# Decode attention: four batches of a kv head interleaved over the partitions in 16 KB runs, P padded with zeros, V loads among the last K loads, w4 in ten loads

## The chip, the cores and the metric

One core of one Trainium2 chip runs the whole program. The time is device microseconds of one execution. Spans in profiles are about 1.7 us shorter than the times. All comparisons are against executions of the kernel before on the same chip in the same rounds, unless a sentence says otherwise. Where one experiment's time is subtracted from another's, the two may come from different chips and rounds; the median of the kernel before lay between 224.1 and 224.8 us in all of them.

Engines are named as the profile names them: PE multiplies matrices, PEld loads its weights, DVE and ACT are the vector and scalar engines, POOL is GpSimd, and SP does nothing here but issue loads, in order.

## The reference, cut to what matters

```python
x  = A_x                                     # [4, 1, 576], bf16
xn = layernorm(x)
# A: 32 query heads, 16 kv heads, Dh = 128, a window of the last 2048 keys, batch 4
q = (xn @ wq) -> [4, 32, 1, 128]
p = softmax(q . k * Dh**-0.5)
A = (p . v) -> [4, 1, 4096] @ wo
# B: a small mixer and MLP: gelu(ln(xn) @ w1), a shift that leaves zeros at S = 1, @ w2,
#    x1 = xn + hs;  B = x1 + gelu(ln(x1) @ w3) @ w4        # w3: 576 x 4608, w4: 4608 x 576
return x + A + B
```

K and V of the window are 33.5 MB each; wq and wo are 4.7 MB each, w3 and w4 5.3 MB each, w1 and w2 together 1.3 MB. Every byte is used once, so this is a kernel of loads: 88.9 MB with the program's own instructions.

## The kernel before

A *unit* is 1 MB of K or V: one kv head, two of the four batches. In a unit, partition `(i, b)` holds 32 successive keys of one batch, which are 8 KB in one piece. K units go through a ring of 7 slots, V units through a ring of 9. SP issues all K units, then V units as slots come free; wo, w1 and w2 go over the dead K ring.

```python
NKU = 7; NVU = 9                  # ring slots of 1 MB
def kv_pairs(ring_t, slot, cache, u):
    g, pr = u // 2, u % 2
    return [(ring_t[:, slot * UE:(slot + 1) * UE],
             cache[pr:B:2, g, Sk - W:Sk, :].rearrange("b (i t) d -> i b (t d)", t=NT))]   # NT = 32
```

PE transposes K in blocks of eight 128x128 tiles (an *evacuation* by DVE or ACT moves each block from PSUM to SBUF). The scores of one kv head are 16 matmuls of 512 columns. The columns of one batch stand at every second place:

```python
# transposes: in_ is loaded as weights, the identity streams past
ins = e.transpose(tb[n % NTB][:, t, :], kring[:, u % NKU, 8 * k + t, :], ident_bf[:])
# scores: batch b in partitions 32b..32b+31 of PSUM, lhsT = the padded queries
ins = e.matmul(Sps[32*b:32*b+32, c4, :]..., lhsT=Qpad[:, g, b, :],
               rhs=ktbuf[:, n % NKT, :, bh:128:2], ...)
```

The exponentials come after the last head, all heads at once, and write P with a step of two, so that one transpose of P gives the layout that the V units have. The zeros between are set once:

```python
P_sb = sb("P_sb", [128, NT, 64, 2], BF16)            # zeroed once, by POOL
e.activation(out=P_sb[s, 8*q:8*q+8, :, bh], in_=Sps[s, q, :]..., func=Exp, ...)   # 8 of 64 x 512
ins = e.transpose(PTps[q][:, t, :], P_sb[:, 8*q+t, :, :].rearrange("p i b -> p (i b)"), ident_bf[:])
```

The w4 matmuls come last, in five groups; the first three wait for 1728, 1728 and 1152 KB of w4.

## Time and profile before

| | |
|---|---|
| time, median | 224.28 us of three executions, one of them an outlier of 335.86 us |
| span of the profile | 223.1 us |
| moved | 88.9 MB |
| K part on PE | 5.39 us per kv head, 19 to 106 us |
| last K transpose (SP then issues wo) to first V product | 104.8 to 119.0 us |
| last w4 matmuls | 209.6 to 220.9 us |

These are lines of the page's second part: 40 equal slices of the span. `PEclk` is the granted clock of PE in tenths, `DMA` the busy share of the 16 DMA engines in tenths (9 is 90% or more), GB/s what they moved.

```profile
PEclk9999999999999999999755555555587555665579
DMA  6999999999999999999999999999999999999950
GB/s 249 426 420 422 420 422 419 420 422 416 419 422 417 417 422 420 420 420 417 422 414 413 412 412 419 422 417 419 420 420 417 422 416 426 419 414 410 409 210 1
```

The DMA never pauses between the first slice and the tail (409 to 426 GB/s), so the time is bytes over rate, plus a start and a tail. Whatever engine waits in the middle costs nothing as long as this row stays full: from 107 to 119 us PE is busy for 4.2 of 12 us, and the DMA moves 417 GB/s.

These are lines of the chain of waits (start in us, duration in us, what): two heads of the K part, and the end.

```profile
30.34 1.09 PE ps L337 x16
...
35.73 1.10 PE ps L337 x15
...
179.78 29.80 DMA vring<-in_B_w_dram
209.57 0.04 issue
209.62 11.28 PE ps L423 x72
```

From 30.34 to 35.73 is one head: 5.39 us, of which the 16 score matmuls (L337) are 1.1. At the end, all 72 w4 matmuls stand behind the first piece of w4.

These are three lines of the timeline of SP (start, time until the last issue of the group, what):

```profile
86.97 7.04 SPq L159 DMA_DIRECT2D vring<-in_A_v_cache_dram  x9
104.75 0.40 SPq L159 DMA_DIRECT2D kring<-in_A_wo_dram  x1
120.00 1.39 SPq L159 DMA_DIRECT2D vring<-in_A_v_cache_dram  x2
```

Nine V loads are issued while the last seven K units are still in their slots. They and wo are what the DMA works on during the softmax.

These are the groups of the exponentials and of the score matmuls (line, engine, operation, shapes, count, busy us, mean ns of one, idle before):

```profile
L337 PE MATMUL ps<-regB,Qpad 128*32 128x512 bf16 x256 | 17.6, 392 | 4.5 <-ACT regB L327 4.5
L363 ACT ACTIVATE P_sb<-ps,negb 64x512 bf16<-64x512 f32 x8 | 6.6, 824 | 2.6 <-DVE negb L358 2.5
```

### The profile page before, as it was taken

To read this page: it belongs to the slowest core of one execution; us is meant where nothing else is said; L and a number is where in the kernel's file an instruction comes from. 1 tells how busy PE (TensorE), PEld (TensorE's weight loads), DVE (VectorE), ACT (ScalarE), POOL (GpSimd) and SP (SyncE) were. 2 spreads that over 40 slices of the span, in tenths; PEclk is the share of its full clock that TensorE was granted. 3 is DMA by queue.
4 is the path that set the end of the run, shared out by engine and by line. 5 is a ranking of instruction groups with operands and counts; after the bars stand their busy time and mean duration, and the time that the engine had idled before them with its cause. 6 is when DMAs were issued, how large, how long until landed. Compare 5 with 4: busy or idle time off the path is not lost.

```text
span 223.1 us, 6242 instructions
## 1 busy us (share of the span) xinstructions
PE 163.6 (73%) x2933; PEld 124.6 (56%) x2934; DVE 70.3 (32%) x124; ACT 62.1 (28%) x76; POOL 7.8 (4%) x14
## 2 busy tenths in 40 slices
PE   0459999999999999997267722665993435997596
PEld 0456777777777777775047722454573434576363
DVE  4803556666666556664441000051000000000000
ACT  2002555555555555555594000000200000000000
POOL 8500000000000000000000000000000000000000
PEclk9999999999999999999755555555587555665579
DMA  6999999999999999999999999999999999999950
GB/s 249 426 420 422 420 422 419 420 422 416 419 422 417 417 422 420 420 420 417 422 414 413 412 412 419 422 417 419 420 420 417 422 416 426 419 414 410 409 210 1
DMA packets 13682, 88.91 MB, mean 399 GB/s; under 512 B 1356, under 2 KB 1752, under 8 KB 4440
## 3 DMA queue, kind: packets, MB, share of 16 engines
q1 hardware_dynamic: 13640, 88.50, 96.1%
q8 instruction: 23, 0.38, 0.7%
q10 hardware_dynamic: 16, 0.01, 0.0%
q14 instruction: 3, 0.02, 0.0%
HBM read 88.49 MB, written 0.00 MB: 397 GB/s over the span
## 4 chain that ended last, share of the span: by engine, by line
DMA 43%; PE 40%; ACT 12%; issue 1%; DVE 1%; SPq 1%
DMA vring<-in_A_v_cache_dram 25%; PE ps L321 23%; DMA vring<-in_B_w_dram 13%; ACT regB L327 8%; PE ps L337 8%; PE ps L423 6%; DMA vring<-in_A_wq_dram 5%; ACT P_sb L363 3%; PE ps L402 2%; PE ps L309 1%; DVE rmax L357 1%; SPq L159 1%; PE ps L372 0%; ACT PT L379 0%; PE ps L294 0%
## 5 line engine op out<-in xcount | busy, mean ns | idle before, releaser
L321 PE MATMUL ps<-ident_bf,kring 128*128 128x128 bf16 x1024 | 66.7, 220 | 0.6 <-ACT regB L327 0.5
L321 PEld LDWEIGHTS ps<-ident_bf,kring 128*128 128x128 bf16 x1024 | 57.9, 98 | 14.1 <-issue 7.8
L328 DVE COPY regB<-ps 128x1024 bf16<-128x1024 bf16 x80 | 52.3, 687 | 36.0 <-PE ps L321 34.3
L327 ACT ACTIVATE regB<-ps 128x1024 bf16<-128x1024 bf16 x48 | 47.5, 1021 | 48.2 <-PE ps L321 48.2
L402 PE MATMUL ps<-PT,vring 128*128 128x4 bf16 x1024 | 30.6, 166 | 29.5 <-DMA vring<-in_A_v_cache_dram 26.7
L402 PEld LDWEIGHTS ps<-PT,vring 128*128 128x128 bf16 x1024 | 28.9, 103 | 33.6 <-DMA vring<-in_A_v_cache_dram 28.5
L337 PE MATMUL ps<-regB,Qpad 128*32 128x512 bf16 x256 | 17.6, 392 | 4.5 <-ACT regB L327 4.5
L513 ACT ACTIVATE h2T_sb<-ps 128x144 bf16<-128x144 f32 x1 | 0.3, 290 | 49.7 <-PE ps L507 49.7
L423 PE MATMUL ps<-kring,ORT 128*4 128x288 bf16 x64 | 13.7, 398 | 0.3 <-DVE ORT L441 0.3
L423 PE MATMUL ps<-vring,h2T_sb 128*4 128x288 bf16 x72 | 11.3, 328 | 2.6 <-DMA vring<-in_B_w_dram 2.6
L437 DVE TENSOR_TENSOR OTn<-ps,rinvB 128x64 bf16<-128x64 f32 (+2 forms) x3 | 0.6, 202 | 39.6 <-PE ps L402 39.6
L337 PEld LDWEIGHTS ps<-regB,Qpad 128*32 128x32 bf16 x256 | 5.3, 94 | 11.1 <-ACT regB L327 5.9
L423 PEld LDWEIGHTS ps<-vring,h2T_sb 128*4 128x4 bf16 x72 | 6.8, 96 | 6.8 <-DMA vring<-in_B_w_dram 2.7
L259 ACT ACTIVATE sd<-mv 4x1 f32<-4x1 f32 x3 | 0.6, 202 | 35.3 <-DVE mv L257 35.3
L423 PEld LDWEIGHTS ps<-kring,ORT 128*4 128x4 bf16 x64 | 7.0, 113 | 5.9 <-DVE ORT L441 0.4
L372 PE MATMUL ps<-ident_bf,P_sb 128*128 128x128 bf16 x32 | 4.1, 309 | 6.6 <-ACT P_sb L363 6.6
L475 DVE TENSOR_TENSOR x_bf<-ps,xn_bf 4x288 bf16<-4x288 f32 x2 | 0.9, 446 | 23.8 <-PE ps L470 23.8
L528 DVE CAST out_sb<-ps 4x288 bf16<-4x288 f32 x1 | 0.4, 446 | 24.0 <-PE ps L423 24.0
L372 PEld LDWEIGHTS ps<-ident_bf,P_sb 128*128 128x128 bf16 x32 | 3.1, 140 | 7.9 <-ACT P_sb L363 7.9
L363 ACT ACTIVATE P_sb<-ps,negb 64x512 bf16<-64x512 f32 x8 | 6.6, 824 | 2.6 <-DVE negb L358 2.5
L273 PE MATMUL ps<-ident_bf,xn_bf 4*128 4x4 bf16 x8 | 0.5, 166 | 8.8 <-DVE ragsrc L266 8.4
L498 PE MATMUL ps<-x1nT,regB 128*128 128x4 bf16 x144 | 5.2, 172 | 1.5 <-DMA regB<-in_B_w_dram 1.5
(78 smaller groups left out, 68.6 us busy)
## 6 DMA issues: line engine op xcount, KB each, us to landing
kring<-in_A_k_cache_dram SPq DMA_DIRECT2D x32, 1024.0 KB, 12.6
vring<-in_A_v_cache_dram SPq DMA_DIRECT2D x32, 1024.0 KB, 21.6
kring<-in_A_wo_dram SPq DMA_DIRECT2D x1, 4608.0 KB, 26.0
regB<-in_B_w_dram SPq DMA_DIRECT2D x4, 1152.0 KB, 27.0
vring<-in_A_wq_dram SPq DMA_DIRECT2D x4, 1024.0 KB, 7.9
vring<-in_B_w_dram SPq DMA_DIRECT2D x2, 1728.0 KB, 30.7
kring<-in_B_w_dram SPq DMA_DIRECT2D x2, 576.0 KB, 13.5
vring<-in_B_w_dram SPq DMA_DIRECT2D x1, 1152.0 KB, 30.2
```

The lines of the kernel that those rows point to most:

```text
L159: e.dma_start(o_, i_).then_inc(S[skey], 16)
L309: ins = e.matmul(ps[:, 4 + (w % NTB), :], lhsT=zeros_bf[:, 0:128], rhs=zeros_bf[:, :], start=True, stop=True)
L321: ins = e.transpose(tb[n % NTB][:, t, :], kring[:, u % NKU, 8 * k + t, :], ident_bf[:])
L327: return "act", lambda e: e.activation(out=ktbuf[:, n % NKT], in_=tb[n % NTB], func=ACTF.Copy)
L328: return "dve", lambda e: e.tensor_copy(out=ktbuf[:, n % NKT], in_=tb[n % NTB])
L337: ins = e.matmul(Sps[32 * b:32 * b + 32, c4, :].rearrange("p (t i) -> p t i", t=8), lhsT=Qpad[:, g, b, :], rhs=ktbuf[:, n % NKT, :, bh:128:2],
L357: add("dve", lambda e: e.tensor_reduce(out=rmax[:], in_=Sps, axis=AX.XY, op=ALU.max), waits=[f"SC{G - 1}"], sig="rmax", key=KS)
L363: add("act", lambda e, q=q, s=s, bh=bh: e.activation(out=P_sb[s, 8 * q:8 * q + 8, :, bh], in_=Sps[s, q, :].rearrange("p (t i) -> p t i", t ...
L372: ins = e.transpose(PTps[q][:, t, :], P_sb[:, 8 * q + t, :, :].rearrange("p i b -> p (i b)"), ident_bf[:])
L402: ins = e.matmul(o_, lhsT=vring[:, u % NVU, t, :], rhs=r_, start=(t == 0), stop=(t == NT - 1))
L423: return e.matmul(ACC[h], lhsT=lhsT, rhs=rhs, start=start, stop=stop)
L498: ins = e.matmul(H2Tps[:, n, :], lhsT=w3main[:, r, lo:hi:st], rhs=x1nT[:, r, :], start=(r == 0 and n == 0), stop=False, skip_group_check=True)
```

## The change

The intent: longer runs for the DMA. One load now brings 2 MB, one kv head of all four batches; a partition holds 64 successive keys, 16 KB in one piece. The rings become 3 and 4 slots of 2 MB. The columns of one batch in the transposed K now stand at every fourth place, and so do the values of one batch in P. To have work for the DMA during the softmax, V0 to V3 are issued among the last K loads. P moves into the space beside the transposed K, so that w3 must wait for the P transposes. w4 comes in pieces of 0.6 MB, each with its own matmuls.

The diff, cut to its core:

```diff
-NKU = 7
-NVU = 9
+NKU = 3
+NVU = 4
+V_EARLY = 4
-    NT = 32
+    NT = 64
+        def kv_src(cache, g):
+            return cache[:, g, Sk - W:Sk, :].rearrange("b (i t) d -> i b (t d)", t=NT)
+        def issue_k(g, key):          # waits for the last transpose of head g - 3
+        def issue_v(g, key):          # waits for PV of head g - 4
+        for g in range(G):
+            issue_k(g, g)
+        for g in range(V_EARLY):
+            issue_v(g, G - V_EARLY + g - 0.5)          # V0 after K11, V1 after K12, ...
+        wo_wait = f"T{8 * (G - 1) + 7}"                # the last K transpose
         ... wo, w1, w2 ...
+        for g in range(V_EARLY, G):
+            issue_v(g, KV + g)
-        ev_w3 = [... [f"SC{G - 1}"] ...]
+        ev_w3 = [... ["PTt7"] ...]                     # after V15 in SP's order
-        W4P = [(0, 3, 0), (3, 6, 2), (6, 8, 4)]
+        for c in range(8):                             # one load and one group of matmuls each
...
-                                       rhs=ktbuf[:, n % NKT, :, bh:128:2],
+                        ins = e.matmul(Sps[32 * b:32 * b + 32, c4, :], lhsT=Qpad[:, g, b, :], rhs=kt[:, b:2048:B],
...
-        for q in range(4):
-            for bh in range(2):              # out=P_sb[s, 8q:8q+8, :, bh], 64 x 512
+        for q in range(2):
+            for b in range(B):               # 32 x 1024
+                    out=P_sb[s, 32 * q:32 * q + 32, :, b], in_=Sps[s, 2 * q:2 * q + 2, :]...
...
-        for q in range(4):                   # P transposes, 32 in 4 groups
+        for q in range(8):                   # 64 in 8 groups
```

More of the change, by code (lines that the diff above doesn't have):

```diff
@@ L19 @@
 N_WARM = 6
-WO_AFTER = 9
-W12_AFTER = 11
+PT_ACT = (5, 7)
 AO_CH = ((0, 4), (4, 7), (7, 8))
@@ L46, in bass_parallel_sum__sliding_block_cached__mixer_s_mlp__decode_kernel @@
     G = Hkv
-    NU = 2 * G
-    NT = 32
+    NT = 64
     UE = NT * 128
-    NHB = 4 * NU
+    NHB = 8 * G
     scale = float(Dh) ** -0.5
@@ L68, in bass_parallel_sum__sliding_block_cached__mixer_s_mlp__decode_kernel @@
         W3E = 4 * F + FH
-        regB_t = sb("regB", [128, max(NKT * 1024, W3E)], BF16)
+        PE_ = 8192
+        regB_t = sb("regB", [128, max(NKT * 1024 + PE_, W3E)], BF16)
+        P_sb = regB_t[:, NKT * 1024:NKT * 1024 + PE_].rearrange("p (t i b) -> p t i b", t=NT, b=B)
         kring = kring_t[:].rearrange("p (s t d) -> p s t d", s=NKU, t=NT)
@@ L114, in bass_parallel_sum__sliding_block_cached__mixer_s_mlp__decode_kernel @@
         negb = sb("negb", [128, 1], FP32)
-        rs4 = sb("rs4", [128, 4], FP32)
+        rs2 = sb("rs2", [128, 2], FP32)
         rsum = sb("rsum", [128, 1], FP32)
@@ L118, in bass_parallel_sum__sliding_block_cached__mixer_s_mlp__decode_kernel @@
         rinvB = sb("rinvB", [128, 128], FP32)
-        P_sb = sb("P_sb", [128, NT, 64, 2], BF16)
         PT = sb("PT", [128, NT, 128], BF16)
@@ L167, in bass_parallel_sum__sliding_block_cached__mixer_s_mlp__decode_kernel @@
         KV = KS + 4.0
-        KT = KV + NU + 8.0
+        KT = KV + 2 * G + 8.0
         P = lambda *a, **k: add("pool", *a, **k)
@@ L177, in bass_parallel_sum__sliding_block_cached__mixer_s_mlp__decode_kernel @@
         P(lambda e: e.memset(Qpad_t[:], 0.0), sig="qpad_zero", key=-96)
-        P(lambda e: e.memset(P_sb[:], 0.0), sig="p_zero", key=-95)
+        P(lambda e: e.memset(P_sb, 0.0), sig="p_zero", key=-95)
         P(lambda e: e.memset(ident_f[:], 1.0), sig="if1", key=-94)
@@ L191, in bass_parallel_sum__sliding_block_cached__mixer_s_mlp__decode_kernel @@
         ev_wq.append(add_dma([(wqrag, rag_src(A_wq))], ("wq", 4), (), -15))
-        def kv_pairs(ring_t, slot, cache, u):
-            g, pr = u // 2, u % 2
-            return [(ring_t[:, slot * UE:(slot + 1) * UE],
-                     cache[pr:B:2, g, Sk - W:Sk, :].rearrange("b (i t) d -> i b (t d)", t=NT))]
-        def last_unit(nslots, s_lo, s_hi):
-            return max(u for u in range(NU) if s_lo <= u % nslots <= s_hi)
-        for u in range(NU):
-            ev_k.append(add_dma(kv_pairs(kring_t, u % NKU, A_k_cache, u), ("k", u % NKU),
-                                [f"T{4 * (u - NKU) + 3}"] if u >= NKU else [], u))
@@ L204, in bass_parallel_sum__sliding_block_cached__mixer_s_mlp__decode_kernel @@
-        wo_wait = f"T{4 * last_unit(NKU, 0, (_o - 1) // UE) + 3}"
-        for u in range(NU):
-            kk = KS + 0.01 * u
-            w = [f"PV{u - NVU}"] if u >= NVU else (["q"] if u < WQ_SLOTS else [])
-            ev_v.append(add_dma(kv_pairs(vring_t, u % NVU, A_v_cache, u), ("v", u % NVU), w, kk))
-            if u == WO_AFTER - 1:
-                ev_wo = add_dma([(wo_sb.rearrange("p h r n -> p h (r n)"), A_wo.rearrange("(h p r) n -> p h (r n)", h=8, r=4))],
-                                "wo", [wo_wait], kk + 0.005)
-            if u == W12_AFTER - 1:
-                ev_w1 = add_dma([(w1main, B_w1[0:512, :].rearrange("(p r) n -> p r n", r=4)), (w1rag, rag_src(B_w1))], "w1",
-                                [wo_wait], kk + 0.005)
-                ev_w2 = add_dma([(w2main, B_w2[0:512, :].rearrange("(p r) n -> p r n", r=4)), (w2rag, rag_src(B_w2))], "w2",
-                                [wo_wait], kk + 0.006)
+        def kv_src(cache, g):
+            return cache[:, g, Sk - W:Sk, :].rearrange("b (i t) d -> i b (t d)", t=NT)
@@ new lines, in issue_k @@
+        def issue_k(g, key):
+            w = [f"T{8 * (g - NKU) + 7}"] if g >= NKU else []
+            ev_k.append(add_dma([(kring_t[:, g % NKU * UE:(g % NKU + 1) * UE], kv_src(A_k_cache, g))], ("k", g % NKU), w, key))
+        def issue_v(g, key):
+            w = [f"PV{g - NVU}"] if g >= NVU else (["q"] if g < WQ_SLOTS else [])
+            ev_v.append(add_dma([(vring_t[:, g % NVU * UE:(g % NVU + 1) * UE], kv_src(A_v_cache, g))], ("v", g % NVU), w, key))
+        for g in range(G):
+            issue_k(g, g)
@@ new lines, in bass_parallel_sum__sliding_block_cached__mixer_s_mlp__decode_kernel @@
+        for g in range(V_EARLY):
+            issue_v(g, G - V_EARLY + g - 0.5)
+        wo_wait = f"T{8 * (G - 1) + 7}"
+        ev_wo = add_dma([(wo_sb.rearrange("p h r n -> p h (r n)"), A_wo.rearrange("(h p r) n -> p h (r n)", h=8, r=4))],
+                        "wo", [wo_wait], KS)
+        ev_w1 = add_dma([(w1main, B_w1[0:512, :].rearrange("(p r) n -> p r n", r=4)), (w1rag, rag_src(B_w1))], "w1", [], KS + 0.1)
+        ev_w2 = add_dma([(w2main, B_w2[0:512, :].rearrange("(p r) n -> p r n", r=4)), (w2rag, rag_src(B_w2))], "w2", [], KS + 0.2)
@@ L217, in bass_parallel_sum__sliding_block_cached__mixer_s_mlp__decode_kernel @@
+        for g in range(V_EARLY, G):
+            issue_v(g, KV + g)
         w3_src = B_w3[0:512, :].rearrange("(p r) n -> p r n", r=4)
-        ev_w3 = [add_dma([(w3main[:, r, :], w3_src[:, r, :])], ("w3", r), [f"SC{G - 1}"], KT + r) for r in range(4)]
-        ev_w3.append(add_dma([(w3rag, rag_src(B_w3))], ("w3", 4), [f"SC{G - 1}"], KT + 4))
+        ev_w3 = [add_dma([(w3main[:, r, :], w3_src[:, r, :])], ("w3", r), ["PTt7"], KT + r) for r in range(4)]
+        ev_w3.append(add_dma([(w3rag, rag_src(B_w3))], ("w3", 4), [], KT + 4))
@@ L224, in bass_parallel_sum__sliding_block_cached__mixer_s_mlp__decode_kernel @@
         ev_w4 = []
-        s4 = (NU - NVU) % NVU
-        assert all((s4 + s_) % NVU + 2 <= NVU for s_ in (0, 2, 4))
-        W4P = [(0, 3, 0), (3, 6, 2), (6, 8, 4)]
-        for n, (c0, c1, s_) in enumerate(W4P):
-            o0 = (s4 + s_) % NVU * UE
-            v = vring_t[:, o0:o0 + (c1 - c0) * 4 * D].rearrange("p (c rn) -> p c rn", c=c1 - c0)
-            ev_w4.append(add_dma([(v, w4_main[:, c0:c1, :])], ("w4", n), [f"PV{NU - NVU + s_ + 1}"], KT + 5 + n))
-            for c in range(c0, c1):
-                for q in range(4):
-                    w4tile[4 * c + q] = v[:, c - c0, q * D:(q + 1) * D]
-        o0 = (s4 + 4) % NVU * UE + 2 * 4 * D
-        assert 2 * 4 * D + 4 * D <= 2 * UE
+        W4N = []
+        for c in range(8):
+            g = G - NVU + c // 3
+            o0 = g % NVU * UE + c % 3 * 4 * D
+            v = vring_t[:, o0:o0 + 4 * D]
+            ev_w4.append(add_dma([(v, w4_main[:, c, :])], ("w4", c), [f"PV{g}"], KT + 5 + c))
+            W4N.append((4 * c, 4 * c + 4))
+            for q in range(4):
+                w4tile[4 * c + q] = v[:, q * D:(q + 1) * D]
+        o0 = (G - NVU + 2) % NVU * UE + 2 * 4 * D
         v3 = vring_t[:, o0:o0 + 3 * D]
         v1 = vring_t[:, o0 + 3 * D:o0 + 4 * D]
-        wl = [f"PV{NU - NVU + 5}"]
-        ev_w4.append(add_dma([(v3, w4_t3)], ("w4", 3), wl, KT + 8))
-        ev_w4.append(add_dma([(v1, w4_t1)], ("w4", 4), wl, KT + 9))
+        ev_w4.append(add_dma([(v3, w4_t3)], ("w4", 8), [], KT + 13))
+        ev_w4.append(add_dma([(v1, w4_t1)], ("w4", 9), [], KT + 14))
         for q in range(3):
@@ L244, in bass_parallel_sum__sliding_block_cached__mixer_s_mlp__decode_kernel @@
         w4tile[35] = v1
-        W4N = [(12 * n, 12 * n + 12) for n in range(2)] + [(24, 32), (32, 35), (35, 36)]
+        W4N += [(32, 35), (35, 36)]
         ev_o = [None, None]
@@ L315, in pe_T @@
         def pe_T(n):
-            u, k = n // 4, n % 4
+            g, k = n // 8, n % 8
             def f(e):
@@ L320, in f @@
                 for t in range(8):
-                    ins = e.transpose(tb[n % NTB][:, t, :], kring[:, u % NKU, 8 * k + t, :], ident_bf[:])
+                    ins = e.transpose(tb[n % NTB][:, t, :], kring[:, g % NKU, 8 * k + t, :], ident_bf[:])
                 return ins
@@ L333, in f @@
                 for c4 in range(4):
+                    n0 = (8 * g + 2 * c4) % NKT
+                    kt = regB_t[:, n0 * 1024:(n0 + 2) * 1024]
                     for b in range(B):
-                        n = 8 * g + 4 * (b % 2) + c4
-                        bh = b // 2
-                        ins = e.matmul(Sps[32 * b:32 * b + 32, c4, :].rearrange("p (t i) -> p t i", t=8), lhsT=Qpad[:, g, b, :],
-                                       rhs=ktbuf[:, n % NKT, :, bh:128:2],
+                        ins = e.matmul(Sps[32 * b:32 * b + 32, c4, :], lhsT=Qpad[:, g, b, :], rhs=kt[:, b:2048:B],
                                        start=(g == 0), stop=(g == G - 1), tile_position=(0, 32 * b))
@@ L343, in bass_parallel_sum__sliding_block_cached__mixer_s_mlp__decode_kernel @@
         for n in range(NHB):
-            w = [ev_k[n // 4]] if n % 4 == 0 else []
+            w = [ev_k[n // 8]] if n % 8 == 0 else []
             if n == 0:
@@ L359, in bass_parallel_sum__sliding_block_cached__mixer_s_mlp__decode_kernel @@
             waits=["rmax"], sig="negb", key=KS + 0.05)
-        for q in range(4):
-            for bh in range(2):
-                s = slice(64 * bh, 64 * bh + 64)
-                add("act", lambda e, q=q, s=s, bh=bh: e.activation(
-                    out=P_sb[s, 8 * q:8 * q + 8, :, bh], in_=Sps[s, q, :].rearrange("p (t i) -> p t i", t=8), func=ACTF.Exp,
-                    bias=negb[s, 0:1], scale=scale, accum_out=rs4[s, q:q + 1]),
-                    waits=["negb", "p_zero"], sig=f"exp{q}" if bh else None, key=KS + 0.1 + 0.01 * q + 0.001 * bh)
+        for q in range(2):
+            for b in range(B):
+                s = slice(32 * b, 32 * b + 32)
+                add("act", lambda e, q=q, s=s, b=b: e.activation(
+                    out=P_sb[s, 32 * q:32 * q + 32, :, b], in_=Sps[s, 2 * q:2 * q + 2, :].rearrange("p c (t i) -> p (c t) i", t=16),
+                    func=ACTF.Exp, bias=negb[s, 0:1], scale=scale, accum_out=rs2[s, q:q + 1]),
+                    waits=["negb", "p_zero"], sig=f"exp{q}" if b == B - 1 else None, key=KS + 0.1 + 0.01 * q + 0.001 * b)
         def pe_PT(q):
@@ L371, in f @@
                 for t in range(8):
-                    ins = e.transpose(PTps[q][:, t, :], P_sb[:, 8 * q + t, :, :].rearrange("p i b -> p (i b)"), ident_bf[:])
+                    ins = e.transpose(PTps[q % 4][:, t, :], P_sb[:, 8 * q + t, :, :].rearrange("p i b -> p (i b)"), ident_bf[:])
                 return ins
             return f
-        for q in range(4):
-            add("pe", pe_PT(q), waits=[f"exp{q}"] + ([f"E{NHB - 1 - k}" for k in range(NTB)] + ["xn2T"] if q == 0 else []),
-                sig=f"PTt{q}", key=KS + 0.2 + 0.01 * q)
-            if q == 3:
-                add("act", lambda e: e.activation(out=PT[:, 24:32, :], in_=PTps[3], func=ACTF.Copy), waits=["PTt3"], sig="PT3", key=KS + 0.3)
+        for q in range(8):
+            w = [f"exp{q // 4}"] + ([f"E{NHB - 1 - k}" for k in range(NTB)] + ["xn2T"] if q == 0 else [])
+            add("pe", pe_PT(q), waits=w + ([f"PT{q - 4}"] if q >= 4 else []), sig=f"PTt{q}", key=KS + 0.2 + 0.01 * q)
+            if q in PT_ACT:
+                add("act", lambda e, q=q: e.activation(out=PT[:, 8 * q:8 * q + 8, :], in_=PTps[q % 4], func=ACTF.Copy),
+                    waits=[f"PTt{q}"], sig=f"PT{q}", key=KS + 0.3 + 0.01 * q)
             else:
-                add("dve", lambda e, q=q: e.tensor_copy(out=PT[:, 8 * q:8 * q + 8, :], in_=PTps[q]), waits=[f"PTt{q}"],
+                add("dve", lambda e, q=q: e.tensor_copy(out=PT[:, 8 * q:8 * q + 8, :], in_=PTps[q % 4]), waits=[f"PTt{q}"],
                     sig=f"PT{q}", key=KS + 0.3 + 0.01 * q)
-        add("dve", lambda e: e.tensor_reduce(out=rsum[:], in_=rs4[:], axis=AX.X, op=ALU.add), waits=["exp3"], sig="rsum", key=KS + 0.5)
+        add("dve", lambda e: e.tensor_reduce(out=rsum[:], in_=rs2[:], axis=AX.X, op=ALU.add), waits=["exp1"], sig="rsum", key=KS + 0.5)
         add("dve", lambda e: e.reciprocal(out=rinv[:], in_=rsum[:]), waits=["rsum"], sig="rinv", key=KS + 0.51)
@@ L387, in bass_parallel_sum__sliding_block_cached__mixer_s_mlp__decode_kernel @@
         add("pe", lambda e: e.matmul(rinvps, lhsT=ones_f[:], rhs=diag[:], start=True, stop=True), waits=["diag", "ones_f"],
-            sig="rinvp", key=KV + 2.5)
+            sig="rinvp", key=KV + 3.5)
         add("dve", lambda e: e.tensor_copy(out=rinvB[:].rearrange("p (g b e) -> p g b e", b=B, e=2),
@@ L391, in bass_parallel_sum__sliding_block_cached__mixer_s_mlp__decode_kernel, with pe_PV @@
             waits=["rinvp"], sig="rinvB", key=KS + 0.6)
-        def pe_PV(u):
-            g, pr = u // 2, u % 2
-            o_ = OTps(g)[:, 8 * g:8 * g + 8].rearrange("p (bh b e) -> p bh b e", bh=2, b=2)[:, :, pr, :]
+        def pe_PV(g):
             def f(e):
@@ L400, in f @@
                 for t in range(NT):
-                    r_ = PT[:, t, :].rearrange("p (bh b r) -> p bh b r", bh=2, b=2)[:, :, pr, 2 * g:2 * g + 2]
-                    ins = e.matmul(o_, lhsT=vring[:, u % NVU, t, :], rhs=r_, start=(t == 0), stop=(t == NT - 1))
-                return ins
-            return f
-        for u in range(NU):
-            add("pe", pe_PV(u), waits=[ev_v[u]] + ([f"PT{q}" for q in range(4)] if u == 0 else []),
-                sig=f"PV{u}", key=KV + u)
+                    r_ = PT[:, t, :].rearrange("p (b r) -> p b r", b=B)[:, :, 2 * g:2 * g + 2]
+                    ins = e.matmul(OTps(g)[:, 8 * g:8 * g + 8].rearrange("p (b e) -> p b e", e=2), lhsT=vring[:, g % NVU, t, :], rhs=r_,
+                                   start=(t == 0), stop=(t == NT - 1))
+                return ins
+            return f
+        for g in range(G):
+            add("pe", pe_PV(g), waits=[ev_v[g]] + ([f"PT{q}" for q in range(8)] if g == 0 else []), sig=f"PV{g}", key=KV + 2 * g + 1)
         def pe_sel(a, z):
@@ L438, in bass_parallel_sum__sliding_block_cached__mixer_s_mlp__decode_kernel @@
                                                            in1=rinvB[:, 16 * a:16 * z], op=ALU.mult),
-                waits=["rinvB", f"PV{4 * z - 1}"], sig=f"OTn{n}", key=kk + 0.2)
+                waits=["rinvB", f"PV{2 * z - 1}"], sig=f"OTn{n}", key=kk + 0.2)
             add("pe", pe_sel(a, z), waits=[f"OTn{n}"] + ([f"ORT{n - 1}"] if n else []), sig=f"sel{n}", key=kk + (0.3 if last else 1.3))
@@ L449, in pe_t1 @@
             return ins
-        KH = KV + 11.5
+        KH = KV + 9.5
         add("pe", pe_t1, waits=["t1", "ident_f"], sig="t1acc", key=KH + 5.1)
```

## The prediction

> **What bounds the kernel now.** The DMA engines. The page's DMA row is at 9 tenths in every slice but the first and the tail, 410 to 426 GB/s: 88.9 MB at 418 GB/s is 213 us of 223.1. In the K part (19 to 106 us in the chain of waits) PE, at 5.39 us per kv head (64 transposes, 16 score matmuls), is slower than the DMA at about 5.0, but nothing is lost: seven K and nine V slots keep the queue full. The softmax gap, 107 to 119 us in the timeline, is hidden too: 105 to 125 us still moves 408 to 421 GB/s. At the end w4 part 0 releases PE at 209.6 us, and 72 matmuls (11.3 us) run to 220.9.
>
> **Gains.**
> 1. Longer runs. Single packets in the trace took 159 ns (4096 B), 181 (4608 B), 312 (8192 B): about 6 ns plus 0.0373 ns per byte. Estimate for 16 KB: 618 ns, against 624 for two of 8 KB. Over all K and V: about 2 us.
> 2. w4 in pieces: its matmuls start about 2 us earlier relative to w3, but the DMA itself finishes only 2 to 3 us before PE today. Worth 1 to 2 us.
>
> **Costs: the DMA queue runs dry.** The SP queue is in order, and K has only three slots of 2 MB.
> - From about K7 each K load waits for its slot (5.39 against 4.95 us per head): 2 us idle.
> - V0 to V3 go between K11 and K15, so K12 to K15 arrive 10 us apart and PE starves: K15 lands near 116 us; today the last K is transposed by 105.8. PE in bursts will partly run at half clock: [...] this trace agrees (1.00 in the K part, 0.50 in the V part).
> - Behind K15 stands wo, which waits for the last transpose, and nothing else is queued: 5 to 8 us of transposes and about 1.5 us from issue to first bytes (first issue 0.81 us; the 0 to 5 us window implies bytes from 2.3). About 9 us idle.
> - wo, w1 and w2 are 15 us of work (6.05 MB). V4 waits for PV0. From the last transpose: eviction and scores 2.5, max 2.5, eight exponentials of 1024 columns at about 1.3 (0.87 now for 512) 10.4, last four groups of P transposes and the copy 5.2 (2.1 now), PV0 2.0, issue 1.5: 24 us. About 8 us idle.
> Total 19 to 20 us of idle DMA, all on the critical path, since from V4 on all is DMA again.
> - The P_sb memset doubles (3.5 to 7 us) and holds the first layernorm's tensor_scalar on DVE (3.51 us today, 0.42 the second time): K starts near 20 us, harmless.
>
> **Prediction.** 224.3 + 20 - 2 - 2 = about 239 us (rounded), range 231 to 246. Faster by over 2%: 0.03; within 2%: 0.07; slower by over 2%: 0.90.
>
> **What would show it.** About 420 GB/s except two holes: one after K15, near 115 to 125 us, one before PV0 ends, near 140 to 148 us; SP waiting on transposes and PV; PV starting near 144 us instead of 119; 16 KB packets at 618 ns; the last w4 matmul about 1 us after its landing.
>
> **What would make it wrong.** 16 KB packets off the line; PE at full clock for K12 to K15 (3 us better); score matmuls slower with a stride of four (8-byte steps), which no view shows; a shorter softmax.

2, 9 and 8 us of idle DMA, 19 to 20 in all, less 2 and 2 for the gains, on 224.3 came to about 239 us. That PE would run partly at half clock in K12 to K15 was an estimate of mine; the trace before has a granted clock of 1.00 in the K part and 0.50 in most of the V part.

## The result, and the profile after

| | before | after |
|---|---|---|
| time, median | 224.77 us | 258.1 us (257.91 to 258.40, 4 runs) |
| ratio | | 1.150, 95% interval 1.145 to 1.155 |
| span of the profile | 223.1 us | 256.5 us |
| K part on PE, per head | 5.39 us | 6.31 us |
| last K transpose (SP then issues wo) | 104.8 us | 131.3 us |
| one exponential and its accumulator read | 0.87 us for 512 columns | 2.52 us for 1024 |
| first V product | 119.0 us | 162.2 us |

A ratio is the mean time of one kernel's fast runs over that of the other's of the same rounds, so it is not quite the ratio of the medians quoted. The 224.77 is the median of four executions with the outlier of 335.86 us among them; the three others have a mean of 224.4, and the ratio is taken against these. The direction was as predicted, the size was not: 33 us longer, where I had said 15.

The same three lines of the page's slices, after:

```profile
PEclk9999999999999999797798555555556855575569
DMA  7999998888889999999039900299999999999991
GB/s 272 420 443 427 416 386 340 327 328 335 327 332 358 416 442 416 439 419 434 28 108 420 405 13 0 82 422 427 429 424 432 422 432 416 430 413 416 410 396 58
```

There are three shortfalls where I had predicted two holes and a trickle. From the sixth slice to the thirteenth the rate is 327 to 386 instead of 420. The two holes, in the 20th and 21st slice and from the 24th to the 26th, are where I had placed them by cause, later and the second twice as long.

The stretches of the trace (stretch, its length, busy us and instructions of PE, PEld, DVE, ACT and POOL, granted clock, DMA share, GB/s) give their size:

```profile
20.00:97.00 77.00, 73.92 (x969) 49.22 (x972) 39.93 (x61) 36.22 (x37) 0.00 (x0) 1.00 0.91 369
120.00:125.00 5.00, 2.07 (x32) 1.58 (x30) 1.47 (x3) 1.84 (x2) 0.00 (x0) 1.00 0.46 193
125.00:130.00 5.00, 5.00 (x60) 3.33 (x58) 2.07 (x3) 1.47 (x2) 0.00 (x0) 0.66 0.00 0
150.00:165.00 15.00, 7.23 (x147) 6.73 (x145) 3.24 (x7) 10.59 (x9) 0.00 (x0) 0.50 0.00 1
170.00:235.00 65.00, 42.70 (x982) 32.48 (x983) 4.80 (x17) 1.72 (x4) 0.00 (x0) 0.58 1.01 426
```

With 425 GB/s as the full rate of the new loads, the K part lost 77 x (1 - 369/425) = 10 us. The first hole is 10 us (2.7 in 120 to 125, 5 in 125 to 130, 2.4 in the next five), the second 17.5 (2.3, 15.0 and 0.3). That is 38 us of idle DMA. The span grew by 33, so about 4 us were gained, as I had summed the gains. The miss lies in the idle time, 38 against 19 us.

The chain of waits, one head of the K part, then K15 landing:

```profile
33.37 2.02 PE ps L332 x16
...
39.68 2.02 PE ps L332 x16
...
101.73 22.64 DMA kring<-in_A_k_cache_dram
```

The 16 score matmuls (now L332) take 2.02 us, 0.92 more than before, with the same arithmetic, the same 512 columns and the same granted clock of 1.00. That is exactly the growth of the head, from 5.39 to 6.31. K15 took 22.6 us from issue to landing, because V3 and other loads stood before it (with V0 to V3 behind K15, in e5, PE waited 0.2 us for K loads in the whole run, against 9.1 us here).

The groups of score matmuls and exponentials after the change:

```profile
L332 PE MATMUL ps<-regB,Qpad 128*32 128x512 bf16 x256 | 32.2, 632 | 3.8 <-ACT regB L322 3.8
L357 ACT ACTIVATE regB<-ps,negb 32x1024 bf16<-32x1024 f32 x8 | 20.1, 2517 | 3.5 <-DVE negb L352 3.4
```

An exponential of twice the columns takes three times as long. The timeline of SP after the change:

```profile
101.73 0.54 SPq L159 DMA_DIRECT2D kring<-in_A_k_cache_dram  x1
131.29 0.40 SPq L159 DMA_DIRECT2D kring<-in_A_wo_dram  x1
164.03 45.60 SPq L159 DMA_DIRECT2D vring<-in_A_v_cache_dram  x12
```

wo is issued when the last transpose is done, and V4 when PV0 is done. From there to the end of the span are 256.5 - 164.0 = 92.5 us. This number returns in every experiment that keeps the order of the loads, so the whole question is when V4 is issued.

### The profile page after: what moved, and what is told of

Read it like the earlier page. It is cut to its first block, busy times and chain, and to the rows that moved or that the text cites. A ratio compares the mean times of both kernels' runs of the same rounds, so it can differ in the third digit from the quotient of the medians.

```text
span 256.5 us, 6269 instructions
## 1 busy us (share of the span) xinstructions
PE 182.7 (71%) x2966; PEld 130.3 (51%) x2966; DVE 75.7 (30%) x127; ACT 76.7 (30%) x77; POOL 11.3 (4%) x14
## 4 chain that ended last, share of the span: by engine, by line
DMA 40%; PE 40%; ACT 15%; SPq 2%; issue 1%; DVE 1%
PE ps L316 18%; DMA kring<-in_A_k_cache_dram 15%; DMA vring<-in_A_v_cache_dram 14%; DMA regB<-in_B_w_dram 11%; PE ps L332 11%; ACT regB L357 8%; ACT regB L322 6%; PE ps L415 5%; PE ps L394 4%; SPq L159 2%; PE ps L366 1%; DVE rmax L351 1%; PE ps L499 1%; ACT PT L373 0%; PE ps L382 0%
## 5 line engine op out<-in xcount | busy, mean ns | idle before, releaser
L316 PE MATMUL ps<-ident_bf,kring 128*128 128x128 bf16 x1024 | 69.8, 225 | 9.5 <-DMA kring<-in_A_k_cache_dram 9.1
L316 PEld LDWEIGHTS ps<-ident_bf,kring 128*128 128x128 bf16 x1024 | 60.4, 101 | 30.8 <-issue 13.9
L394 PE MATMUL ps<-PT,vring 128*128 128x8 bf16 x1024 | 29.2, 168 | 22.1 <-DMA vring<-in_A_v_cache_dram 20.9
L332 PE MATMUL ps<-regB,Qpad 128*32 128x512 bf16 x256 | 32.2, 632 | 3.8 <-ACT regB L322 3.8
L357 ACT ACTIVATE regB<-ps,negb 32x1024 bf16<-32x1024 f32 x8 | 20.1, 2517 | 3.5 <-DVE negb L352 3.4
L366 PE MATMUL ps<-ident_bf,regB 128*128 128x128 bf16 x64 | 7.2, 313 | 19.3 <-ACT regB L357 19.3
L366 PEld LDWEIGHTS ps<-ident_bf,regB 128*128 128x128 bf16 x64 | 6.7, 149 | 20.5 <-ACT regB L357 20.5
L332 PEld LDWEIGHTS ps<-regB,Qpad 128*32 128x32 bf16 x256 | 6.1, 106 | 16.8 <-issue 12.0
L415 PE MATMUL ps<-kring,ORT 128*4 128x288 bf16 x64 | 12.6, 377 | 0.3 <-DVE ORT L433 0.3
L376 DVE COPY PT<-ps 128x1024 bf16<-128x1024 bf16 x6 | 4.2, 692 | 19.7 <-PE ps L366 19.7
L178 POOL MEMSET regB<- 128x8192 bf16 x1 | 6.9, 6915 | 0.0
```

Source lines behind the costliest of these rows:

```text
L178: P(lambda e: e.memset(P_sb, 0.0), sig="p_zero", key=-95)
L316: ins = e.transpose(tb[n % NTB][:, t, :], kring[:, g % NKU, 8 * k + t, :], ident_bf[:])
L332: ins = e.matmul(Sps[32 * b:32 * b + 32, c4, :], lhsT=Qpad[:, g, b, :], rhs=kt[:, b:2048:B], start=(g == 0), stop=(g == G - 1), tile_posit ...
L357: add("act", lambda e, q=q, s=s, b=b: e.activation(out=P_sb[s, 32 * q:32 * q + 32, :, b], in_=Sps[s, 2 * q:2 * q + 2, :].rearrange("p c (t ...
L366: ins = e.transpose(PTps[q % 4][:, t, :], P_sb[:, 8 * q + t, :, :].rearrange("p i b -> p (i b)"), ident_bf[:])
L376: add("dve", lambda e, q=q: e.tensor_copy(out=PT[:, 8 * q:8 * q + 8, :], in_=PTps[q % 4]), waits=[f"PTt{q}"], sig=f"PT{q}", key=KS + 0.3 + ...
```

## The experiments

**Theory A.** The mechanism of the prediction is right: the SP queue is in order, three K slots are few, K15 is late, and nothing stands behind it. Only two terms were mis-sized, both for one reason, a step of four elements (8 bytes) where the kernel before had two (4 bytes): the read of the score matmuls, and the write of the exponentials. **Rivals.** B: the 16 KB packets themselves are slow, or the ring alone explains it. C: the exponentials are slow because they use 32 partitions, or because one reads two PSUM banks.

A caution about results: the comparison with the reference called every run correct, even the one that is wrong (e2). Why it sees no error in e2 was not looked into; perhaps the attention term is too small in the output. So the mended layouts below rest on index arithmetic, given with each, and not on the comparison.

### e1: the score matmuls read runs of 32

The transpose of K streams an identity past the loaded tile (a step of 64 in the tile of the P transposes, in e4, lengthens their weight loads, 176 against 149 ns after the change, and not the matmuls, 314 against 313), so a permuted identity permutes the columns of the result for nothing (64 transposes take 4.14 us with either, where PE does not wait). Column `32 b + i` of the new matrix has its one in row `4 i + b`, which is the partition of key group i of batch b. The scores come out in the same order as before.

```diff
+        pv_ = perm_bf[:].rearrange("p (b i) -> p b i", b=B)
+        affine_select(out=pv_, in_=pv_, fill=0.0, pattern=[[-1, B], [-B, 32]], channel_multiplier=1)
-   e.transpose(tb[n % NTB][:, t, :], kring[:, g % NKU, 8 * k + t, :], ident_bf[:])
+   e.transpose(tb[n % NTB][:, t, :], kring[:, g % NKU, 8 * k + t, :], perm_bf[:])
-   rhs=kt[:, b:2048:B]
+   rhs=kt.rearrange("p (t b i) -> p b t i", t=16, b=B)[:, b]
```

> The K transposes use a permuted identity, so that the score matmuls read runs of 32 columns in place of every fourth column; the result stays right. Theory A (two of my terms were mis-sized: the stride-4 read of the score matmuls, which makes a group of 16 take 2.02 us instead of 1.10, and the exponentials, 2.52 us each instead of 1.3): a group falls to about 1.1 us, the K period from 6.31 to 5.39 us per kv head, the last K transpose moves from 131 to about 122 us, and the time falls by 8 to 10 us to about 249 us. Rival B (the K ring of three slots alone, or slower 16 KB packets, holds the K part): the group time falls but the period stays above 6 us and the total stays within 2 us of 258.

Measured: 249.06 us (248.07 to 250.51), ratio 1.112 (1.107 to 1.117). A group of 16 score matmuls takes 1.05 us, the period of a head is 5.34 us, and wo is issued at 122.74 us instead of 131.29. All three numbers of theory A hold; rival B falls for this term. From V4's issue (154.2) to the end of the span (246.3) are 92.1 us.

### e2: the steps one by one (wrong on purpose)

Heads 0 to 3 read with step 4, the next four with step 2, then step 1, then runs of 32. The eight exponentials write with eight patterns.

```diff
+   r_ = (kt[:, b:2048:B], kt[:, b % 2:1024:2], kt[:, 512*b:512*b+512], <runs of 32>)[g // 4]
+   exponentials of 1024: out step 4 | step 2 | step 1 | runs of 32;  of 512: step 4 | 2 | 1 | 8
```

> Result wrong on purpose; one look. The score matmuls read their 512 columns with step 4 in heads 0 to 3, step 2 in heads 4 to 7, step 1 in heads 8 to 11 and runs of 32 in heads 12 to 15; the eight exponentials write with different steps, four of 1024 columns (step 4, step 2, step 1, runs of 32) and four of 512 columns (step 4, 2, 1, 8). Theory A1 (an 8-byte step is the cost): step 4 takes 2.0 us per 16 score matmuls, the other three 1.1 us; an exponential of 1024 columns takes 2.5 us with step 4 and about 1.3 us with the three others, and of 512 columns about 1.3 us with step 4 and 0.87 us with step 2 and step 1. Rival A2 (the 32 partitions, or the two PSUM banks read by one instruction, make the exponential slow): all four of 1024 columns take about 2.5 us whatever the step.

Measured, one look, so the state of the run is unknown; the durations are of single instructions of one trace. The timeline of PE, one group of each pattern in the order step 4, step 2, step 1, runs of 32:

```profile
45.19 2.02 PE L337 MATMUL ps<-regB,Qpad 128*32 128x512 bf16 x16 [0.22 <-ACT regB L322]
51.50 1.09 PE L337 MATMUL ps<-regB,Qpad 128*32 128x512 bf16 x16 [0.22 <-ACT regB L322]
73.06 1.05 PE L337 MATMUL ps<-regB,Qpad 128*32 128x512 bf16 x16 [0.22 <-ACT regB L322]
91.43 1.05 PE L337 MATMUL ps<-regB,Qpad 128*32 128x512 bf16 x16
```

The timeline of ACT, the four exponentials of 1024 columns in the order of the diff (the accumulator reads between them are left out):

```profile
131.40 2.51 ACT L372 ACTIVATE regB<-ps,negb 32x1024 bf16<-32x1024 f32 x1 [2.45 <-DVE negb L357]
...
133.93 1.39 ACT L372 ACTIVATE regB<-ps,negb 32x1024 bf16<-32x1024 f32 x1
...
135.38 1.10 ACT L372 ACTIVATE regB<-ps,negb 32x1024 bf16<-32x1024 f32 x1
...
136.58 1.11 ACT L372 ACTIVATE regB<-ps,negb 32x1024 bf16<-32x1024 f32 x1
```

The four of 512 columns that follow take 1.39 us (step 4), 0.83 (step 2), 0.68 (step 1) and 2.52 (step 8).

Theory A holds, and rival C falls: on the same 32 partitions and the same two banks, 1024 columns take 1.10 us in one piece and 2.51 with step 4. The two sizes give the cost of one more column: 0.82 ns at step 1, 1.09 at step 2, 2.19 at step 4 (differences of the 1024 and the 512 column times, over 512). For the writes of ACT even step 2 is not free (1.39 against 1.10 us for 1024 columns). For the reads of the matmuls step 2 nearly is (1.09 against 1.05 us), and step 4 nearly doubles the time (2.02 us). Runs of 32 and step 4 read out of the same stretch of 2048 columns (1.05 and 2.02 us), so the length of the stretch is not the cause.

### e3: exponentials in runs of 32, alone

A first version with P in the order `(t, b, i)` did not build. So P is laid out as `(i, b, t)`: an exponential writes runs of 32 along t, and the transpose loads its columns with a step of 64, in the order `(i, b)` that the V loads have. The exponential now reads its scores in steps.

```diff
-   P_sb = ....rearrange("p (t i b) -> p t i b", t=NT, b=B)
+   P_sb = ....rearrange("p (i b t) -> p i b t", t=NT, b=B)
-   out=P_sb[s, 32 * q:32 * q + 32, :, b], in_=Sps[...].rearrange("p c (t i) -> p (c t) i", t=16)
+   out=P_sb[s, :, b, 32 * q:32 * q + 32], in_=Sps[...].rearrange("p c (t i) -> p i (c t)", t=16)
-   in_=P_sb[:, 8 * q + t, :, :].rearrange("p i b -> p (i b)")
+   in_=P_sb[:, :, :, 8 * q + t].rearrange("p i b -> p (i b)")
```

> Only the layout of P changes: each exponential writes runs of 32 and reads its scores in step instead, and the P transposes load their columns with a step of 64; the result stays right. Theory A: an exponential takes 1.1 to 1.3 us instead of 2.52, the time from the last K transpose to the first V product falls from 31 to about 21 us, the hole in the DMA before V4 shrinks by the same 10 us, and the time falls to about 248 us. Rival: another wait opens (the stepped reads of scores or of P cost as much), and the time stays above 254 us.

Measured: three fast runs of 245.88 to 247.97 us (the median with the slow one is 247.46), ratio 1.102 (1.097 to 1.107). The profiled run was a slow one (250.48 us), so no stage times are compared from it, but the instructions are plain: an exponential takes 1.11 us. Theory A holds.

### e4: both strides out

> Both strides taken out at once (permuted identity for K, runs of 32 for P). Theory A: these two terms are all that my sum had wrong, so the time is what I predicted for the change, 239 us, plus or minus 2; the two DMA holes behind K15 and before V4, 15 to 17 us together, stay. Rival: the queue order was mis-sized as well, and the time lies outside 236 to 242 us.

Measured: 239.58 us (238.54 to 241.70), ratio 1.070 (1.064 to 1.076). These are its groups of score matmuls and exponentials, two lines of SP, and the K part in the stretches of the trace:

```profile
L337 PE MATMUL ps<-regB,Qpad 128*32 128x512 bf16 x256 | 18.4, 412 | 2.9 <-ACT regB L327 2.7
L362 ACT ACTIVATE regB<-ps,negb 32x1024 bf16<-32x1024 f32 x8 | 8.8, 1105 | 2.6 <-DVE negb L357 2.5
```

```profile
124.47 0.39 SPq L160 DMA_DIRECT2D kring<-in_A_wo_dram  x1
145.56 45.69 SPq L160 DMA_DIRECT2D vring<-in_A_v_cache_dram  x12
```

```profile
20.00:97.00 77.00, 69.62 (x1024) 52.98 (x1023) 42.20 (x65) 38.10 (x38) 0.00 (x0) 0.96 1.00 400
```

The time is the number that I had predicted for the change, and the trace shows how far each term agrees. Against the same 425 GB/s the K part (the line above) loses 4.5 us, the hole behind K15 9.4 (265 GB/s from 110 to 135 us) and the hole before V4 6.6 (331 from 135 to 165); predicted were 2, 9 and 8. So the two holes are right with the strides out, 16 us together, and the exact agreement of the total is partly luck: 2.5 us too little in the K part stand against 1.4 too much before V4. The two effects, e1 (258.1 - 249.1 = 9.0 us) and e3 (11.2, from its three fast runs, whose mean is 246.9), add up to 20.2; together they took 18.5. wo is issued at 124.5 (predicted: K15 at 116 and 5 to 8 us of transposes), V4 21.1 us later (predicted 22.5 without the start of the transfer). The rest of the change, 15 us slower than before, is the order of the loads and the ring.

### e5: V0 to V3 behind K15, strides as in the change

```diff
-            issue_v(g, G - V_EARLY + g - 0.5)
+            issue_v(g, G + 0.1 * g)          # after K15, before wo
```

> Strides as in the change; only V0 to V3 are issued after K15 and before wo, not among the last K loads. Theory A (K15 is late because four V loads of 5 us stand before it, and the queue is empty behind it): PE isn't starved any more, the last K transpose comes at about 121 instead of 131 us, the hole behind K15 closes, a hole of about 5 us stays before V4, and the time falls by 8 to 11 us to about 248 us. Rival (the early V loads only fill time that the K ring leaves idle, and their place matters little): within 3 us of 258.

Measured: 247.25 us (247.08 to 248.16), ratio 1.104 (1.101 to 1.107). wo is issued at 120.3 us, V4 at 153.0. The hole behind K15 is gone: the page gives 407 GB/s or more for the slices from 104 to 141 us, and one hole before V4.

```profile
GB/s 262 423 442 427 363 382 326 379 327 347 342 339 315 336 350 347 315 419 430 430 407 416 409 91 0 363 427 427 427 427 422 425 425 427 418 422 413 408 384 47
```

Theory A holds for the time, the end of the K part and the first hole. One part of it failed: the hole before V4 is 12 us (156 GB/s from 141 to 160 us) and not about 5. The rival is true in part too: without the early V loads the K part loses 15 us (348 GB/s from 20 to 104 us), 5 more than in the change. The early V loads did fill idle time, but they delayed K15 by more than that was worth.

### e6: all three mends

> Both strides out and the V loads after K15. Theory A: only the K ring of three slots still costs DMA time, about 5 to 8 us idle between 35 and 100 us, offset by the gains of the longer runs and of w4 in pieces; the time is 224 to 228 us, within 2% of the kernel before. Rival: over 232 us, which would mean a cost in the change that neither the strides nor the order explain.

Measured: 226.01 us (224.77 to 226.78), ratio 1.008 (1.003 to 1.012). As expected, all but 2 of the 33 us are gone. What is left of the idle time is in the K part, which the trace shows at 402 GB/s and not at 425 (4 us; 5 to 8 were expected):

```profile
20.00:97.00 77.00, 73.40 (x1138) 56.10 (x1136) 46.47 (x71) 42.55 (x43) 0.00 (x0) 1.00 0.99 402
```

### e7: V0 moved up to fill that gap

```diff
+            issue_v(g, 9.5 if g == 0 else G + 0.1 * g)      # on top of e6
```

> As the run with all three mends, but V0 is issued after K9 and only V1 to V3 after K15, so that one 2 MB load fills the time that the three-slot K ring leaves idle. Theory A: the rate between 35 and 95 us rises from about 400 to 420 GB/s, and the time falls by 2 to 4 us against 226, to 222 to 224. Rival (the K ring costs nothing any more): the same 226 us.

Measured: 227.64 us median, of which four of six runs count as slow, since they are over 1.5% above the fastest (223.79); ratio of the two fast ones 1.003 (0.997 to 1.010). This expectation failed; the two fast runs (223.79 and 226.58) can't be told from e6. The profiled run is a slow one (granted clock 0.804, against 0.810 and 0.815 in the fast ones). It shows PE waiting 3.8 us for a K load at 78.9 us and wo issued at 112.8 us, 7 us later than in e6. That reads as PE starved by the load of 5 us in front of a K load, in small what the change did four times. But no fast run of e7 was profiled, so why it brought nothing is argued and not shown.

### e8: w4 in pieces, alone, on the kernel before

```diff
-        W4P = [(0, 3, 0), (3, 6, 2), (6, 8, 4)]
+        W4P = [(c, c + 1, 2 * (c // 3)) for c in range(8)]      # one load and one group of matmuls each
```

> The kernel before, with only the w4 part of the change: nine pieces and the last row block, each matmul group waiting for its own piece. My prediction gave this part 1 to 2 us: the first w4 matmul starts about 2 us earlier, just after the second gelu, and the time is 222 to 223.5 us. Rival: the wait for the first piece was hidden, and the time is within 0.5 us of before.

Measured: 222.60 us (222.47 to 222.75), ratio 0.992 (0.989 to 0.994). The timeline of PE at the end:

```profile
207.12 7.75 PE L424 MATMUL ps<-vring,h2T_sb 128*4 128x288 bf16 x48 [0.47 <-ACT h2T_sb L514]
215.12 1.14 PE L424 MATMUL ps<-vring,h2T_sb 128*4 128x288 bf16 x8 [0.26 <-DMA vring<-in_B_w_dram]
216.52 2.22 PE L424 MATMUL ps<-vring,h2T_sb 128*4 128x288 bf16 x16 [0.25 <-DMA vring<-in_B_w_dram]
```

The first w4 matmul starts at 207.1 us, when the gelu is done, and not at 209.6. From 215 us on PE waits for the DMA (0.26 and 0.25 us), so little more can be had from smaller pieces. This part of the change is a gain, of the size predicted.

### e9 and e10: w3 before V4, and PE kept busy

e9 takes e7's order and loads all of w3 between w2 and V4, and moves its matmuls and the second gelu into the V part. e10 adds six matmuls of zeros after PV12, PV13 and PV14.

```diff
-        ev_w3 = [... ["PTt7"], KT + r) ...]
+        ev_w3 = [... ["PTt7"] if r > 1 else ["SC15"], KS + 0.3 + 0.1 * r) ...]
-   add("pe", pe_h2(r), ..., key=KT + r)
+   add("pe", pe_h2(r), ..., key=KH + 8 + 0.01 * r)
```

> As the run with V0 after K9, and all of w3 is loaded between w2 and V4, with its matmuls and the second gelu moved into the V part; result right. Theory A (the DMA is the limit, and what PE does after the last byte is all that can still be cut): the 12.7 us of w3 cover the softmax, the tail after the last byte shrinks because the w4 matmuls start as their pieces land, and the time is 218 to 221 us, faster than before by 1.5 to 2.5%. Rival: PE at half clock takes longer for 72 matmuls than the DMA for w4, and the time stays at 221 to 223 us.

> As the run before this one, with six matmuls of zeros after each of PV12, PV13 and PV14, into a bank that nobody reads, so that PE stays busy before the w4 matmuls. If the half clock holds the tail, the granted clock in the last 12 us is 1.0 and the time falls by 1 to 2 us; if the DMA is the limit there, it changes by less than 0.7 us.

Measured: e9 228.65 us (225.98 to 230.22), ratio 1.015 (1.010 to 1.020); e10 229.03 (224.51 to 230.81), ratio 1.004 (0.999 to 1.010), with runs of both kinds in each. The expectation of e9 failed. That of e10 is undecided: its fast runs have a mean of 225.4 us, 2.4 less than those of e9 (227.8), but the median of its six runs is 0.4 us above that of e9. Both profiled runs are slow ones, so what follows is what these two traces show, and not an explanation of the times. They carry the order of e7 (wo at 113.8 us in e9). And in e9 the work of PE in the V part, now with the w3 matmuls, ends so late that all w4 matmuls stand together behind the last V product: the last 80 matmuls (8 of wo, 72 of w4) take 11.6 us from 214.7 us on, so the rival named the place, though not the time. In e10 the granted clock is 1.00 from 210 us, and the same 80 run from 215.3 to 225.3 us, shorter by 1.6 us but begun 0.6 later. Whether the zeros help in a run without e7's order stays open.

### e11: all three mends and four K slots

```diff
-NKU = 3
+NKU = 4                                     # on top of e6
```

> As the run with all three mends (strides out, V0 to V3 after K15; 226.0 us), with a K ring of four slots instead of three. Theory A: the 402 GB/s of its K part (20 to 97 us) rise to about 420, which is worth 3 us, and the time is 222 to 224 us, equal to or a little faster than the kernel before. Rival (the lower rate there comes from the 16 KB runs and not from waits for slots): the rate and the time stay.

Measured: 221.14 us (220.74 to 221.47), ratio 0.987 (0.983 to 0.991). The same stretch as in e6:

```profile
20.00:97.00 77.00, 73.40 (x1134) 56.42 (x1136) 46.46 (x71) 42.28 (x43) 0.00 (x0) 1.00 1.01 425
```

The rate is 425 GB/s, above the 420 of the kernel before in the same stretch. So the missing 5% in e6 was waiting for slots, and the first half of rival B is refuted: 16 KB runs are not slow. This version is faster than the changed kernel by 37 us, and than the one before by 3.0 us: 1.3%, clear of noise. Of these 3.0 us e8 had 1.8 from w4 in pieces alone, so about 1.2 are left for the longer runs and everything else.

### e12: the change as it is, with four K slots

> The change as it is, strides and V order included, but with four K slots instead of three. Theory A: the K period stays 6.31 us because PE sets it, but loads run one head further ahead, so that the V loads among the last K loads no longer starve PE: the last K transpose comes at about 121 to 123 instead of 131 us, the softmax hole stays 18 us or so, and the time falls to 247 to 251 us. Rival (the stride of the score matmuls alone explains the late end of the K part): within 3 us of 258.

Measured: 252.22 us (251.60 to 254.58), ratio 1.127 (1.121 to 1.134). The last transpose and V4 come at 124.6 and 157.4 us. The direction is theory A's, the size is 1 to 2 us short of it: PE still waits 3.6 us for K15, which lands at 117.7 us. The ring alone is worth 6 us of the 33, so the second half of rival B, the ring as the whole cause, is refuted too; four slots do not replace the other mends.

### The sum

| run | strides out | V0-V3 | K slots | wo issued | V4 issued | span | time |
|---|---|---|---|---|---|---|---|
| after | none | among K | 3 | 131.3 | 164.0 | 256.5 | 258.1 |
| e12 | none | among K | 4 | 124.6 | 157.4 | 249.9 | 252.2 |
| e1 | scores | among K | 3 | 122.7 | 154.2 | 246.3 | 249.1 |
| e5 | none | behind K15 | 3 | 120.3 | 153.0 | 245.5 | 247.3 |
| e4 | both | among K | 3 | 124.5 | 145.6 | 238.2 | 239.6 |
| e6 | both | behind K15 | 3 | 105.8 | 126.9 | 224.2 | 226.0 |
| e11 | both | behind K15 | 4 | 106.0 | 127.1 | 219.3 | 221.1 |

e3, e7, e9 and e10 are left out because their profiled runs are slow ones. In the first five rows the span is V4's issue plus 92.1 to 92.6 us. The last row fits too (92.2). Only e6 does not (97.3): there the DMA had lost its time earlier, in the K part, and still had loads to work off when V4 was issued.

## Why the prediction was right or wrong

- **What bounds the kernel before: right.** The DMA row is full there. The runs of the table are slower or faster by the DMA time they lose or gain; e8 gains in the tail instead.
- **"The DMA queue runs dry", behind K15 and before V4: right in mechanism and place.** e5 removes the first hole, e3 and e4 shorten the second, e6 and e11 close them but for a microsecond or so.
- **The failing steps are two terms of the sum.** First, "5.39 against 4.95 us per head: 2 us idle". I took the head's period over from the kernel before. It was 6.31, since the score matmuls with a step of four took 2.02 us per head instead of 1.10. The K part lost 10 us of DMA time instead of 2, and the last transpose came at 131 us instead of 121 to 124. The stride is not all of this term: with the old period (e4) the K part still lost 4.5 us. I had let the waits for slots begin "from about K7"; SP waited for a transpose 14 times after the change, which is for wo and for each K load from K3 on, and a fourth slot (e11) brings the K part back to 425 GB/s. I had named this step among the things that could make me wrong and had put no time to it. Second, "eight exponentials of 1024 columns at about 1.3, 10.4". They took 2.54 us each with the gaps, 20.3 in all, since their writes have the same step. I had kept the cost of a column from the 512 columns with step two, and for step two the 1.3 us were about right (1.39 in e2). These two strides, measured by e1 and e3 at 9.0 and 11.2 us and together by e4 at 18.5, are the miss of 19 us to about a microsecond; e4, without them, took 239.6 us for a predicted 239, in which the short K term and the long hole before V4 partly cancel.
- **What in the chip makes the step cost this much: not shown.** Against step one, with a step of four the reads of the matmuls take 2.02 and not 1.05 us, the writes of ACT 2.51 and not 1.10 (e2). The runs give the cost and not its cause.
- **PE at half clock in K12 to K15: partly right.** It was an estimate of mine; in the trace before the granted clock is 1.00 in the K part and 0.50 in most of the V part (0.57 on average from 130 to 200 us). The trace after shows a granted clock of 0.66 to 0.67 in three stretches of 5 us between 105 and 130 us and 0.99 or more in the stretches between them. PE had waited 3.2, 2.8 and 2.9 us for K13, K14 and K15 before them; how long a wait it takes to lower the clock was not tested. For K15 this is about 1.7 us (an estimate, 5 us times 1 - 0.66); I had put 3 us on it.
- **Longer runs, "about 2 us": right, a little low per packet.** A 16 KB packet took 611 ns (median) where I had estimated 618, against 624 for two of 8 KB. (The mean, with a few slow packets in it, was 631 after the change and 620 in e11, against 630 for two of 8 KB.) In e11 the DMA moves 425 GB/s from 20 to 97 us and 424 from 130 to 200; before it moved 420 and 419 in the same stretches. K and V are 67.1 MB, 160 us at 419 GB/s, and 1.2% of that is 1.9 us, an estimate; no run changed the length of the runs alone.
- **w4 in pieces, "1 to 2 us": right.** e8 measured 1.8 us.
- **The longer memset: right.** POOL's memset of P took 6.92 us and held DVE's tensor_scalar for 6.77 (3.50 and 3.51 before); PE began with K at 20.6 us, when K0 landed. The two run side by side in the trace (memset 4.22 to 11.14 us, tensor_scalar 4.53 to 11.30); in the trace before, a tensor_scalar of the same shape took 0.42 us at 10.3 us, when POOL had nothing left to do. By what the memset holds it, the trace doesn't show.

## What to carry to other kernels

When a change alters an access pattern, cost each instruction that reads or writes through it anew: the same columns took about twice as long at a step of 8 bytes (2.02 against 1.05 us for 16 score matmuls), and neither the instruction count nor the shapes show it. A permuted identity in a transpose that is needed anyway puts the columns in order for nothing (4.14 us for 64 transposes with either). In an in-order load queue, judge a place by what stands behind it: a load that needs a late event should have others after it that need nothing, and a load placed in front of the one that everybody waits for delays them all. V0 to V3 behind K15 (e5) kept 407 GB/s or more to 141 us, where the change had a hole of 10 us, and took the time from 258.1 to 247.3 us.

## What the runs measured, in short

- A step of four bf16 elements (e2): 16 score matmuls took 2.02 us against 1.05 and 1.09 at step one and two, and an exponential of 1024 columns 2.51 us against 1.10 at step one.
- A column of an ACT write by its step (e2): 0.82 ns at step 1, 1.09 at 2, 2.19 at 4; 512 columns at step 8 took 2.52 us; runs of 32 cost the same as one piece (1.11 against 1.10 us).
- In the K part 64 of 80 matmuls are transposes (the profile calls them MATMUL), and the granted clock is 1.00 from 20 to 97 us before the change, after it and in e11.
- 64 transposes took 4.14 us with the plain and with the permuted identity. The P transposes' weight loads with a step of 64 took 176 ns on average in e4, against 149 contiguous after the change, both at a granted clock of about 0.5.
- A packet on one engine, medians: 159 ns for 4 KB, 181 for 4.5 KB and 312 for 8 KB before the change, 611 for 16 KB after it.
